# Centring instead of normalising the first four tiles, and moving the queries of chunk 0 to chunk 2, in a linear-attention block with a gated feed-forward network

## The chip, the cores and the metric

The kernel runs on one core of one Trainium2 chip. The metric is the device time of one execution in microseconds (us), and the median over several executions is quoted. The core has these engines: TensorE (PE in the profile, with its weight loads listed apart as PEld), VectorE (DVE), ScalarE (ACT), GpSimd (POOL) and SyncE (SP), whose queue starts almost all the DMA transfers here. The time before the change was 224.95 us (median of 3 runs, 224.90 to 224.96).

## The reference

```python
def reference(A_x, A_wqkv, A_wo, B_x, B_w1, B_w2):     # B_x is not used
    x = A_x                                   # (1, 2048, 640), bf16
    xn = _layernorm(x)                        # (x - mean) / sqrt(var + 1e-5)
    # A: linear attention, 32 heads of 20
    q, k, v = split(xn @ wqkv)                # wqkv (640, 1920)
    phi = lambda t: where(t > 0, t + 1, exp(t)) + 1e-6
    pq, pk = phi(q), phi(k)
    kv  = einsum("bhsd,bhse->bhde", pk, v)
    z   = sum over s of pk
    num = einsum("bhqd,bhde->bhqe", pq, kv)
    den = einsum("bhqd,bhd->bhq", pq, z) + 1e-6
    s   = (num / den) @ wo
    # B: feed-forward network (FFN), 1728 hidden features
    g   = silu(relu(xn @ w1) @ w2)            # w1 (640, 1728), w2 (1728, 640)
    return x + s * g
```

## The kernel before

The 2048 rows of x are 16 tiles of 128 rows, and four tiles make a chunk of 512 rows, so there are four chunks, 0 to 3. TensorE needs the normalised rows with features on the partitions, so each tile is transposed. Tiles 0 to 3 are transposed by TensorE itself in the start, because that is quicker than a DMA. The other tiles are transposed by a DMA. TensorE does three kinds of work on a chunk:

- A query block is five matmuls of 512 columns, and there are five such blocks (640 features). The map phi is applied while the result leaves PSUM: an exponential on ScalarE, then work on VectorE.
- An FFN block is also five matmuls of 512 columns. There are 13 of them, and a last half block of 64 features that two chunks share. Its ReLU is a single ScalarE pass.
- A key block is ten matmuls of 320 columns for one tile of the next chunk. Its evacuation is two ScalarE passes and two VectorE operations; then GpSimd adds the keys to a running sum (`zacc`).

The start normalises tile 0 by way of ScalarE's square root, and tiles 1 to 3 by way of a power on GpSimd:

```python
    def LN_norm(t, then=None):
        last_norm[0] = sc.op("DVE", lambda eng: eng.tensor_scalar(
            out=xn[:, t, :], in0=xin[:, t % XR, :], scalar1=mv[:, t, 0:1], scalar2=rsy[:, t:t + 1],
            op0=ALU.subtract, op1=ALU.mult), R=[("xin", t % XR), ("mv", t), ("rsy", t)], W=[("xn", t)])
        # ... cut: a hook, and the load of tile t + 8

    LN_stat(0, 0); LN_stat(0, 1); LN_aggr(0)
    LN_root_act(0)                       # sqrt on ScalarE
    # ... cut: a dummy Exp on ScalarE, so that its table is loaded early
    LN_stat(1, 0)
    LN_recip(0)
    LN_norm(0, late_loads)
    transposes(0, 4)                     # five transposes by TensorE into PSUM bank 4
    warm(11)                             # dummy matmuls that keep TensorE busy
    xnT_copy(0, 4)                       # ScalarE evacuates them
    LN_stat(1, 1); LN_aggr(1)
    LN_root_pool(1)                      # add and pow on GpSimd
    LN_norm(1)
    LN_stat(2, 0)
    K_mm(0, 0, range(0, KS))             # first part of the key block of tile 0
    transposes(1, 5)
    # ... cut: the same for tiles 2 and 3
```

A query block has two forms of evacuation. In chunk 0 (`j == 0`) ScalarE makes two passes; in the others VectorE reads PSUM itself:

```python
    def Q_block(j, f):
        b = nextb()                      # one of six PSUM banks, in turn
        # ... cut: five matmuls into ps[b]
        sc.op("ACT", ... exp: e_ <- ps[b])
        if j == 0:
            sc.op("ACT", ... relu: r_ <- ps[b])
            sc.op("DVE", ... e_ <- min(e_, 1) + 1e-6)
            sc.op("DVE", ... pqT <- e_ + r_)
            return
        sc.op("DVE", ... r_ <- max(ps[b], 0) + 1e-6)
        sc.op("DVE", ... pqT <- min(e_, 1) + r_)          # scalar_tensor_tensor
```

The chunks run their blocks in one fixed order:

```python
    for j in range(J):
        blocks = [("q", f) for f in range(C)] + [("h", f) for f in range(NF)]
        for n, (kind, f) in enumerate(blocks):
            # ... cut: Q_block or H_block; statistics and norms of the next chunk
            if j + 1 < J:
                if n in (8, 11, 14, 17):
                    t = t0 + (n - 8) // 3
                    K_mm(t, 0)           # key blocks always use PSUM banks 0 and 1
                    K_ev(t, 0)
            else:                        # chunk 3: the sum of the keys and the denominators
                if n == 2: z_split()     # GpSimd
                if n == 7: z_col()       # ten tiny matmuls, then VectorE
                if n == 9:
                    den(); H_half(0); H_half(1)
```

After chunk 3 come 160 matmuls that multiply the normalised rows with the keys (called the product G below), then the second FFN layer and the output. The change hardly touches that part.

## Time and profile before

The profile that came with the kernel was taken in a slow execution. The next fence shows its page: the span, and the shares of the chain of waits that ended last.

```profile
span 464.2 us, 3501 instructions
...
PE 98%; issue 1%; DVE 0%
```

Its chain of waits in order of time shows the pace of TensorE (start, duration, what, count).

```profile
42.47 2.94 PE psT L442 x10
...
45.58 6.83 PE psT L520 x14
```

The execution took 465.64 us against 224.95 us timed. Ten key matmuls (L442) took 2.94 us. In a second profile of the same kernel, which was taken later in the study, they took 1.36 us. The clock column of the slow profile nonetheless read 1.00. Everything that a fast TensorE has to wait for is hidden there. The readings below therefore come from the second profile, which the prediction did not have. That execution took 224.89 us.

| reading (second profile of before) | value |
|---|---|
| span | 223.4 us |
| chunk 0 blocks begin / chunk 1 begins / product G begins | 14.04 / 38.90 / 111.87 us |
| a matmul of 320 / 512 columns, back to back | 0.1358 / 0.2155 us |
| from the product G to the end of the span | 111.55 us |

### The profile page before, as it was taken

The page shows a single profiled execution, that of the slowest core. Times are in us where ns is not written, and L with a number is a line of the kernel's source. Part 1 is how long each engine was busy: PE and PEld are TensorE (multiplying, and loading weights), DVE is VectorE, ACT ScalarE, POOL GpSimd, SP SyncE. Part 2 cuts the span into 40 slices and gives each one's busy share as a digit, 9 for nine tenths or more (in the row PEclk, how much of TensorE's full clock was granted, in tenths as well). Part 3 has the DMA queues.
Part 4 walks back from the last instruction along what each step waited for, and adds up shares of the span by engine and source line. Part 5 has one row for each costly group of instructions (what it writes and reads, how often), then busy time and mean ns, then how long its engine had stood idle before and what let it go on. Part 6 is the DMA issues. An engine that isn't in the chain of part 4 may idle for free.

```text
span 464.2 us, 3501 instructions
## 1 busy us (share of the span) xinstructions
PE 457.0 (98%) x1452; PEld 204.5 (44%) x1462; DVE 99.4 (21%) x192; ACT 91.0 (20%) x146; POOL 44.6 (10%) x63
## 2 busy tenths in 40 slices
PE   9999999999999999999999999999999999999997
PEld 7533333333333333333355556455545554554553
DVE  5580103710064001603000001420202020211141
ACT  4542323232332233222200000220010001001000
POOL 3260111111121112200000002000000000000000
DMA  7850000110002000005496006000000000000020
GB/s 242 287 133 25 1 0 0 34 23 1 1 14 42 0 1 0 0 1 120 105 316 189 0 0 227 0 0 1 29 0 30 0 28 1 28 0 30 0 71 14
DMA packets 24333, 23.18 MB, mean 50 GB/s; under 512 B 9006, under 2 KB 23678, under 8 KB 24318
## 3 DMA queue, kind: packets, MB, share of 16 engines
q1 hardware_dynamic: 24174, 22.88, 16.8%
q8 instruction: 11, 0.18, 0.2%
q10 hardware_dynamic: 144, 0.08, 0.1%
q14 instruction: 4, 0.03, 0.0%
HBM read 15.75 MB, written 5.24 MB: 45 GB/s over the span
## 4 chain that ended last, share of the span: by engine, by line
PE 98%; issue 1%; DVE 0%
PE psT L781 26%; PE psT L520 26%; PE psT L714 10%; PE psT L442 10%; PE psT L497 10%; PE psT L820 9%; PE psT L370 1%; PE psT L742 1%; PE psT L805 1%; PE psT L759 1%; PE psT L533 1%; PE psT L727 1%; PE psT L425 1%; PE psT L619 1%; DVE reg L808 0%
## 5 line engine op out<-in xcount | busy, mean ns | idle before, releaser
L781 PE MATMUL psT<-reg,hT 128*128 128x320 bf16 x416 | 123.3, 502 | 0.3
L520 PE MATMUL psT<-reg 128*128 128x512 bf16 x252 | 120.5, 677 | 2.1 <-issue 2.1
L781 PEld LDWEIGHTS psT<-reg,hT 128*128 128x128 bf16 x416 | 61.2, 148 | 60.4 <-issue 17.8
L520 PEld LDWEIGHTS psT<-reg 128*128 128x128 bf16 x260 | 38.5, 149 | 78.8 <-issue 75.6
L442 PE MATMUL psT<-reg 128*128 128x320 bf16 x160 | 50.2, 504 | 0.0
L524 ACT ACTIVATE hT<-psT 128x512 bf16<-128x512 f32 x52 | 31.0, 597 | 83.8 <-PE psT L520 83.8
L497 PE MATMUL psT<-reg 128*128 128x512 bf16 x98 | 46.6, 679 | 0.6 <-issue 0.6
L714 PE MATMUL psT<-reg 128*128 128x320 bf16 x160 | 46.9, 503 | 0.0
L820 PE MATMUL psT<-reg,pqT 128*128 128x320 bf16 x140 | 42.2, 503 | 0.0
L777 ACT ACTIVATE reg<-psT 128x640 bf16<-128x640 f32 x16 | 10.8, 702 | 149.1 <-PE psT L781 82.2
L834 DVE TENSOR_TENSOR reg<-psT,reg 128x640 bf16<-128x640 f32 x14 | 11.5, 824 | 118.0 <-PE psT L820 118.0
L442 PEld LDWEIGHTS psT<-reg 128*128 128x128 bf16 x160 | 23.1, 146 | 26.2 <-issue 13.7
L714 PEld LDWEIGHTS psT<-reg 128*128 128x128 bf16 x160 | 23.9, 150 | 23.1 <-issue 7.5
L454 POOL TENSOR_TENSOR zacc<-zacc,reg 128x640 f32<-128x640 f32 x16 | 22.5, 1406 | 104.9 <-DVE reg L473 104.6
L820 PEld LDWEIGHTS psT<-reg,pqT 128*128 128x128 bf16 x140 | 20.6, 147 | 20.3 <-issue 6.2
L497 PEld LDWEIGHTS psT<-reg 128*128 128x128 bf16 x100 | 15.2, 152 | 30.1 <-issue 29.4
L471 DVE TENSOR_SCALAR ek<-ek 128x640 bf16<-128x640 bf16 x16 | 5.2, 323 | 102.9 <-ACT ek L459 102.9
L810 POOL TENSOR_TENSOR reg<-reg 128x320 bf16<-128x320 bf16 x1 | 0.8, 788 | 178.3 <-DVE reg L808 178.3
L504 ACT ACTIVATE er<-psT 128x512 bf16<-128x512 f32 x20 | 11.9, 597 | 30.1 <-PE psT L497 30.1
L730 DVE TENSOR_TENSOR reg<-psT,mh 120x120 bf16<-120x120 f32 (+1 forms) x6 | 1.6, 269 | 75.4 <-PE psT L727 75.4
L459 ACT ACTIVATE ek<-psT 128x640 bf16<-128x640 f32 x16 | 11.3, 704 | 30.5 <-PE psT L442 30.5
L386 DVE BATCH_NORM_STATS2 stats<-reg 128x6 f32<-128x320 bf16 x32 | 14.1, 479 | 2.0 <-DMA reg<-in_A_x_dram 2.0
(64 smaller groups left out, 180.8 us busy)
## 6 DMA issues: line engine op xcount, KB each, us to landing
reg<-in_A_x_dram SPq DMA_DIRECT2D x16, 160.0 KB, 5.4
rden_by_feature<-rden SPq DMA_DIRECT2D x4, 640.0 KB, 8.7
reg<-rden_by_feature SPq DMA_DIRECT2D x5, 512.0 KB, 10.1
reg<-in_A_x_dram SPq DMA_DIRECT2D x4, 640.0 KB, 6.2
reg<-in_B_w_dram SPq DMA_DIRECT2D x2, 1120.0 KB, 7.1
out_dram<-reg SPq DMA_DIRECT2D x14, 160.0 KB, 1.8
reg<-in_B_w_dram SPq DMA_DIRECT2D x1, 1040.0 KB, 10.5
reg<-in_B_w_dram SPq DMA_DIRECT2D x1, 960.0 KB, 8.7
```

The costliest lines, as they stand in the source:

```text
L386: sc.op("DVE", lambda eng: eng.bn_stats(stats[:, t, a, :], xin[:, t % XR, HN * a:HN * (a + 1)]), R=[("xin", t % XR)], W=[("stats", t, a)])
L442: fns.append(lambda eng, a=a, k=k: eng.matmul(ps[b + a][:, 0:HN], lhsT=xnT[:, k, tok(t)], rhs=wqk[:, k, D + HN * a:D + HN * (a + 1)], star ...
L454: sc.op("POOL", lambda eng: eng.tensor_tensor(out=zacc[:, :], in0=zacc[:, :], in1=pk[:, t, :], op=ALU.add), R=[("zacc",), ("pk", t)], W=[( ...
L459: sc.op("ACT", lambda eng: eng.activation(out=e_.rearrange("p (a n) -> p a n", a=2), in_=ps2(b, HN), func=ACTF.Exp), R=[("ps", b), ("ps", ...
L497: sc.group("PE", [(lambda eng, k=k: eng.matmul(ps[b], lhsT=wqk[:, k, P * f:P * (f + 1)], rhs=xnT[:, k, schunk(j)], start=(k == 0), stop=(k ...
L504: sc.op("ACT", lambda eng: eng.activation(out=e_, in_=ps[b], func=ACTF.Exp), R=[("ps", b)], W=[("er_e", es)])
L520: a = sc.group("PE", [(lambda eng, k=k: eng.matmul(ps[b], lhsT=w1_sb[:, k, P * f:P * (f + 1)], rhs=xnT[:, k, schunk(j)], start=(k == 0), s ...
L524: sc.op("ACT", lambda eng: eng.activation(out=hT[:, f, schunk(j)], in_=ps[b], func=ACTF.Relu), R=[("ps", b)], W=[("hT", j, f)])
L714: fns.append(lambda eng, t=t, a=a: eng.matmul(ps[b + a][:, 0:HN], lhsT=xn[:, t, P * k:P * (k + 1)], rhs=pk[:, t, HN * a:HN * (a + 1)], sta ...
L781: fns = [(lambda eng, u=u, t=t, f=f, n=n: eng.matmul(ps[bs[n] + u][:, 0:HN], lhsT=hT[:, f, tok(t)], rhs=w2_sb[:, f, HN * n:HN * (n + 1)], ...
L820: sc.group("PE", [(lambda eng, c=c, a=a: eng.matmul(ps[b + a][:, 0:HN], lhsT=pqT[:, c, tok(t)], rhs=wf[:, c, HN * a:HN * (a + 1)], start=( ...
L834: sc.op("DVE", lambda eng: eng.tensor_tensor(out=tmpo[:, os_, lo:hi].rearrange(shp, a=na), in0=src, in1=g_sb[:, t, lo:hi].rearrange(shp, a ...
```

## The change

There are two ideas. First, LayerNorm's division by the standard deviation scales each row by one positive number, so it can be applied after a matmul. Tiles 0 to 3 are only centred before they are transposed, which needs the mean alone. The scale goes into the evacuation of their keys (a scale operand of ScalarE's activation) and, since ReLU keeps positive factors, into the silu of the gate. Second, the queries of chunk 0 need the exponential of fully normalised values and are shared by a whole chunk, so they cannot be scaled that way. They are moved to the end of chunk 2, after tiles 0 to 3 have been normalised and transposed a second time by DMA. Chunk 0 begins with FFN blocks instead. TensorE's matmuls stay the same, apart from six fewer dummies.

```diff
     def late_loads(gate):
-        w_load(wqk[:, :, 0:D], A_wqkv[:, 0:D], ("wq",), extra=[gate])
-        # x tiles 4 to 7, then w1 in two parts
+        for i, (f0, f1) in enumerate(FCUT):                    # w1 in three parts, the first at once
+            w_load(w1_sb[:, :, f0:f1], B_w1[:, f0:f1], ("w1", i), extra=[gate])
+            if i == 0: ...                                     # then x tiles 4 to 7
+        w_load(wqk[:, :, 0:D], A_wqkv[:, 0:D], ("wq",))         # query weights last
+    def LN_center(t):
+        return sc.op("DVE", lambda eng: eng.tensor_scalar(
+            out=xn[:, t, :], in0=xin[:, t % XR, :], scalar1=mv[:, t, 0:1], scalar2=None, op0=ALU.subtract), ...)
+    def K_act(t, b, u, func, key):                             # keys: exp and relu
+        sca, Rs = (rsy[:, t:t + 1], [("rsy", t)]) if t < 4 else (1.0, [])
+        sc.op("ACT", ... activation(..., func=func, scale=sca))
@@ Q_block
-        if j == 0:                                             # the form with two ScalarE passes
-            ...
-            return
@@ the start
-    LN_root_act(0); (dummy Exp); LN_stat(1, 0); LN_recip(0); LN_norm(0, late_loads)
-    transposes(0, 4); warm(11); xnT_copy(0, 4)
-    LN_stat(1, 1); LN_aggr(1); LN_root_pool(1); LN_norm(1); LN_stat(2, 0)
-    K_mm(0, 0, range(0, KS)); transposes(1, 5); xnT_copy(1, 5)
-    ...
+    LN_root(0); late_loads(LN_center(0))                       # the root is off the path now
+    transposes(0, 4); warm(8); xnT_copy(0, 4)
+    LN_stats(1); LN_center(1)
+    transposes(1, 5); xnT_copy(1, 5); K_mm(0, 0, range(0, KS))
+    LN_stats(2); LN_center(2); warm(2)
+    K_mm(1, 2, range(0, KS)); transposes(2, 4); xnT_copy(2, 4)
+    K_mm(0, 0, range(KS, C)); K_exp(0, 0)
+    ...
@@ the chunks
-        blocks = [("q", f) for f in range(C)] + [("h", f) for f in range(NF)]
+    qb = [[], [1], [2, 0], [3]]
+        blocks = [("q", qb[j][0], f) for f in range(C) if j > 0] + [("h", j, f) for f in range(NF)]
+        blocks += [("q", qj, f) for qj in qb[j][1:] for f in range(C)]
+        kat = (6, 8, 10, 12) if j == 0 else (8, 11, 14, 17)    # places of the key blocks
+                    if 8 <= n < 12: LN_norm(n - 8)              # chunk 0: tiles 0 to 3 normalised now
                 if n == 9:
                     den()
-                    H_half(0)
                     H_half(1)
+        if j == 1:
+            H_half(0)
+            for t in range(4): xnT_dma(t)                       # and transposed again
-            if j == 0 and n == 12: ...                             # the load of wv
+            if j == 1 and n == 12: ...                             # one chunk later
@@ silu: with a per-row scale, one tile at a time, for pairs with a tile of 0 to 3
```

More of the change, by code (lines that the diff above doesn't have):

```diff
@@ L339, in bass_recurrent_scan__linear_attn_block__dense_activation_relu__prompt_kernel @@
     KS = 3
+    FCUT = [(0, 4 * P), (4 * P, 9 * P), (9 * P, FF)]
     x_load(0)
@@ L347, in late_loads @@
     def late_loads(gate):
-        w_load(wqk[:, :, 0:D], A_wqkv[:, 0:D], ("wq",), extra=[gate])
-        for t in range(4, XR):
-            x_load(t)
-        F1 = 7 * P
-        w_load(w1_sb[:, :, 0:F1], B_w1[:, 0:F1], ("w1", 0))
-        w_load(w1_sb[:, :, F1:FF], B_w1[:, F1:FF], ("w1", 1))
+        for i, (f0, f1) in enumerate(FCUT):
+            w_load(w1_sb[:, :, f0:f1], B_w1[:, f0:f1], ("w1", i), extra=[gate])
+            if i == 0:
+                for t in range(4, XR):
+                    x_load(t)
+        w_load(wqk[:, :, 0:D], A_wqkv[:, 0:D], ("wq",))
     sc.op("POOL", lambda eng: eng.memset(ident[:], 0.0), W=[("ident",)])
@@ L391, in LN_aggr, with LN_root @@
               R=[("stats", t, 0), ("stats", t, 1)], W=[("mv", t)])
-    def LN_root_pool(t):
+    def LN_root(t):
         sc.op("POOL", lambda eng: eng.tensor_scalar(out=rsv[:, t:t + 1], in0=mv[:, t, 1:2], scalar1=EPS_LN,
@@ L397, in LN_root_pool @@
                                                     op=ALU.pow), R=[("rsv", t), ("mhalf",)], W=[("rsy", t)])
-    def LN_root_act(t):
-        sc.op("ACT", lambda eng: eng.activation(out=rsv[:, t:t + 1], in_=mv[:, t, 1:2], func=ACTF.Sqrt,
-                                                bias=epsv[:, :]), R=[("mv", t), ("epsv",)], W=[("rsv", t)])
-    def LN_recip(t):
-        sc.op("DVE", lambda eng: eng.reciprocal(rsy[:, t:t + 1], rsv[:, t:t + 1]), R=[("rsv", t)], W=[("rsy", t)])
+    def LN_center(t):
+        return sc.op("DVE", lambda eng: eng.tensor_scalar(
+            out=xn[:, t, :], in0=xin[:, t % XR, :], scalar1=mv[:, t, 0:1], scalar2=None, op0=ALU.subtract),
+            R=[("xin", t % XR), ("mv", t)], W=[("xn", t)])
     def LN_stats(t):
@@ L409, in LN_stats @@
         LN_aggr(t)
-        LN_root_pool(t)
+        LN_root(t)
     last_norm = [None]
@@ L455, in z_add @@
               R=[("zacc",), ("pk", t)], W=[("zacc",)])
+    def K_act(t, b, u, func, key):
+        o_ = ek[:, t % NEK, u, :]
+        sca, Rs = (rsy[:, t:t + 1], [("rsy", t)]) if t < 4 else (1.0, [])
+        sc.op("ACT", lambda eng: eng.activation(out=o_.rearrange("p (a n) -> p a n", a=2), in_=ps2(b, HN), func=func,
+                                                scale=sca),
+              R=[("ps", b), ("ps", b + 1)] + Rs, W=[(key, t % NEK)])
     def K_exp(t, b):
-        e_ = ek[:, t % NEK, 0, :]
-        sc.op("ACT", lambda eng: eng.activation(out=e_.rearrange("p (a n) -> p a n", a=2), in_=ps2(b, HN), func=ACTF.Exp),
-              R=[("ps", b), ("ps", b + 1)], W=[("ek_e", t % NEK)])
+        K_act(t, b, 0, ACTF.Exp, "ek_e")
     def K_relu(t, b):
-        r_ = ek[:, t % NEK, 1, :]
-        sc.op("ACT", lambda eng: eng.activation(out=r_.rearrange("p (a n) -> p a n", a=2), in_=ps2(b, HN), func=ACTF.Relu),
-              R=[("ps", b), ("ps", b + 1)], W=[("ek_r", t % NEK)])
+        K_act(t, b, 1, ACTF.Relu, "ek_r")
     def K_fin(t):
@@ L504, in Q_block @@
         sc.op("ACT", lambda eng: eng.activation(out=e_, in_=ps[b], func=ACTF.Exp), R=[("ps", b)], W=[("er_e", es)])
-        if j == 0:
-            sc.op("ACT", lambda eng: eng.activation(out=r_, in_=ps[b], func=ACTF.Relu), R=[("ps", b)], W=[("er_r", es)])
-            sc.op("DVE", lambda eng: eng.tensor_scalar(out=e_, in0=e_, scalar1=1.0, scalar2=1e-6, op0=ALU.min, op1=ALU.add),
-                  R=[("er_e", es)], W=[("er_e", es)])
-            sc.op("DVE", lambda eng: eng.tensor_tensor(out=pqT[:, f, schunk(j)], in0=e_, in1=r_, op=ALU.add),
-                  R=[("er_e", es), ("er_r", es)], W=[("pqT", j, f)])
-            return
         sc.op("DVE", lambda eng: eng.tensor_scalar(out=r_, in0=ps[b], scalar1=0.0, scalar2=1e-6, op0=ALU.max, op1=ALU.add),
@@ L522, in H_block @@
                                                          start=(k == 0), stop=(k == C - 1))) for k in range(C)],
-                     R=[("w1", 0 if f < 7 else 1)] + [("xnT", 4 * j + q) for q in range(4)], W=[("ps", b)])
+                     R=[("w1", 0 if f < 4 else 1 if f < 9 else 2)] + [("xnT", 4 * j + q) for q in range(4)], W=[("ps", b)])
         sc.op("ACT", lambda eng: eng.activation(out=hT[:, f, schunk(j)], in_=ps[b], func=ACTF.Relu),
@@ L535, in H_half @@
                     start=(k == 0), stop=(k == C - 1)))
-        a = sc.group("PE", fns, R=[("w1", 1)] + [("xnT", 8 * jp + q) for q in range(8)], W=[("ps", b)])
+        a = sc.group("PE", fns, R=[("w1", 2)] + [("xnT", 8 * jp + q) for q in range(8)], W=[("ps", b)])
         sc.op("ACT", lambda eng: eng.activation(out=hTl[:, jp, :], in_=ps[b], func=ACTF.Relu),
@@ L544, in bass_recurrent_scan__linear_attn_block__dense_activation_relu__prompt_kernel @@
     LN_aggr(0)
-    LN_root_act(0)
-    sc.op("ACT", lambda eng: eng.activation(out=junk[:, :], in_=epsv[:, :], func=ACTF.Exp), R=[("epsv",)], W=[("junk",)])
-    sc.allow_unread.add(("junk",))
-    LN_stat(1, 0)
-    LN_recip(0)
-    LN_norm(0, late_loads)
+    LN_root(0)
+    late_loads(LN_center(0))
     transposes(0, 4)
-    warm(11)
+    warm(8)
     xnT_copy(0, 4)
-    LN_stat(1, 1)
-    LN_aggr(1)
-    LN_root_pool(1)
-    LN_norm(1)
-    LN_stat(2, 0)
-    K_mm(0, 0, range(0, KS))
+    LN_stats(1)
+    LN_center(1)
     transposes(1, 5)
     xnT_copy(1, 5)
-    LN_stat(2, 1)
-    LN_aggr(2)
-    LN_root_pool(2)
+    K_mm(0, 0, range(0, KS))
+    LN_stats(2)
+    LN_center(2)
     warm(2)
+    K_mm(1, 2, range(0, KS))
+    transposes(2, 4)
+    xnT_copy(2, 4)
     K_mm(0, 0, range(KS, C))
@@ L568, in bass_recurrent_scan__linear_attn_block__dense_activation_relu__prompt_kernel @@
     LN_stats(3)
-    LN_norm(2)
-    warm(3)
-    K_mm(1, 2, range(0, 2))
-    transposes(2, 4)
-    xnT_copy(2, 4)
-    LN_norm(3)
-    K_mm(1, 2, range(2, C))
+    LN_center(3)
+    K_mm(1, 2, range(KS, C))
+    K_mm(2, 6, range(0, 2))
     transposes(3, 5)
@@ L578, in bass_recurrent_scan__linear_attn_block__dense_activation_relu__prompt_kernel @@
     K_relu(0, 0)
-    K_mm(2, 6)
+    K_mm(2, 6, range(2, C))
     K_exp(1, 2)
@@ L635, in bass_recurrent_scan__linear_attn_block__dense_activation_relu__prompt_kernel @@
     lastW1 = None
+    qb = [[], [1], [2, 0], [3]]
     for j in range(J):
-        blocks = [("q", f) for f in range(C)] + [("h", f) for f in range(NF)]
-        for n, (kind, f) in enumerate(blocks):
+        blocks = [("q", qb[j][0], f) for f in range(C) if j > 0] + [("h", j, f) for f in range(NF)]
+        blocks += [("q", qj, f) for qj in qb[j][1:] for f in range(C)]
+        kat = (6, 8, 10, 12) if j == 0 else (8, 11, 14, 17)
+        for n, (kind, bj, f) in enumerate(blocks):
             if kind == "q":
-                Q_block(j, f)
+                Q_block(bj, f)
             else:
-                lastW1 = H_block(j, f)
+                lastW1 = H_block(bj, f)
             if j + 1 < J:
@@ L653, in bass_recurrent_scan__linear_attn_block__dense_activation_relu__prompt_kernel @@
                         xnT_dma(7)
+                    if 8 <= n < 12:
+                        LN_norm(n - 8)
                 else:
@@ L659, in bass_recurrent_scan__linear_attn_block__dense_activation_relu__prompt_kernel @@
                         xnT_dma(t0 + n // 2)
-                if n in (8, 11, 14, 17):
-                    t = t0 + (n - 8) // 3
+                if n in kat:
+                    t = t0 + kat.index(n)
                     K_mm(t, 0)
@@ L676, in bass_recurrent_scan__linear_attn_block__dense_activation_relu__prompt_kernel @@
                     den()
-                    H_half(0)
                     H_half(1)
-            if j == 0 and n == 12:
+            if j == 1 and n == 12:
                 w_load(wv_sb[:, :, :], A_wqkv[:, 2 * D:3 * D], ("wv",))
+        if j == 1:
+            H_half(0)
+            for t in range(4):
+                xnT_dma(t)
     for a in range(2):
@@ L775, in silu @@
         def silu(n):
+            dv = [divs[c] for c in sorted({v // S for t in (t0, t1) for v in (D * t, D * t + D - 1)})]
+            if t0 < 4:
+                for u, t in enumerate((t0, t1)):
+                    sca, Rs = (rsy[:, t:t + 1], [("rsy", t)]) if t < 4 else (1.0, [])
+                    sc.op("ACT", lambda eng, u=u, t=t, sca=sca: eng.activation(
+                        out=g_sb[:, t, HN * n:HN * (n + 1)], in_=ps[bs[n] + u][:, 0:HN], func=ACTF.Silu, scale=sca),
+                        R=[("ps", bs[n] + u)] + Rs, W=[("g", t, n)], extra=dv)
+                return
             go = g_sb[:, t0:t0 + 5:4, HN * n:HN * (n + 1)]
             sc.op("ACT", lambda eng: eng.activation(out=go, in_=ps2(bs[n], HN), func=ACTF.Silu),
-                  R=bk(n), W=[("g", t0, n), ("g", t1, n)], extra=[divs[c] for c in sorted({v // S for t in (t0, t1) for v in (D * t, D * t + D - 1)})])
+                  R=bk(n), W=[("g", t0, n), ("g", t1, n)], extra=dv)
         for n in range(2):
```

## The prediction

> **What bounds the kernel now.** The page's chain of waits is TensorE for 98% of the 464.2 us profiled span. But the profiled execution took 465.64 us against 224.95 us timed. In its timeline ten 320-column matmuls take 2.94 us and fourteen 512-column ones 6.71 us, near 1.2 GHz pace, clock column 1.00. So the profile hides waits that only a fast TensorE meets; I halve TensorE and keep other engines, DMA landings and waits.
>
> Summing columns over the groups (no dummy matmuls or transposes) gives about 493,000. The Trainium skill, "TensorE: Matmul & The Clock Gate", section "Back-to-back issue gap", gives N/2.4 + 2.5 ns; some 1,300 matmuls make an estimated 209 us. The profile is slower, so no trace here confirms this. Of 225 us only about 16 are left: the start, a 3.2 us tail (last matmul to end), few stalls. TensorE's real work stays, so only the start can be won.
>
> **Start, before (timeline).** Tile 0's mean is there at 4.10, then root (0.29) and reciprocal (0.16), normalised at 5.11, transposed at 5.33, evacuated 6.14-6.84. Tile 1 waits 1.00 us of VectorE idle for the GpSimd root (rsv 0.23, pow 0.57), tile 3 waits 0.72; tiles 1 to 3 are normalised at 7.20, 9.69 and 10.86. Halving TensorE in this order by hand, first key matmuls at 7.0, key stage done near 14.2. Loads land in time: key weights 7.7, query 11.9, FFN 16.6 and 19.6.
>
> **After.** Centring needs the mean alone: tiles 0 to 3 near 4.55, 6.1, 7.95, 9.5. Tile 0 gains little, because the 38 dummy matmuls run to 5.3-5.5. The sqrt table load leaves (1.28 us twice becomes once; the skill, "ScalarE: Activation LUTs", "What ACT_TABLE_LOAD costs", says 1283 ns, and the trace agrees); it should run before any data, since the old one did not wait for its input. Tiles 1 to 3 no longer wait for GpSimd, and six dummy matmuls go. By hand the key stage ends near 13.1: minus 1.1 us, all critical.
>
> FFN blocks first in chunk 0: one 0.60 us ScalarE pass per 1.09 us block, instead of 1.19 us ScalarE plus VectorE work that stretched to 1.5 us an operation beside GpSimd's zacc adds (28-34 us). Eight banks mostly hid this; I give 0.4 us. First FFN weights should land by 11.
>
> Costs: ten query blocks in a row from chunk 2 into 3, VectorE 1.38 us each against 1.09: a lag of 3-5 us, held by six banks, 0-0.5 us exposed. Eight two-tile gates become sixteen half ones (0.70 becomes two of 0.44 plus); ScalarE idles there. Four 0.45 us normalisations and four transposing DMAs (2.6 us) fall in slack. Total costs 0.2.
>
> **Predicted: 223.7 us, range 222.4 to 225.0.** Faster by over 2%: 0.05; within 2%: 0.93; slower: 0.02.
>
> **What would show it.** Centring within 0.1 us after each mean, no VectorE wait on the GpSimd root in tiles 0-3; one table load before the first evacuation; last key matmuls of tile 3 earlier; TensorE never waiting at chunk 0's first FFN block or at chunk 3's start. The profile, with slow TensorE, may show less or another gain than the timed runs.
>
> **What would make it wrong.** The table load landing between transposes and first evacuation (+1.3 us); fewer dummy matmuls leaving TensorE at a slow clock longer (+1 us or more); the ten-query run stalling TensorE by several us; or chunk 0's query evictions having stalled the old kernel more than I think, a larger gain (to -3 us).

## More of the kernel before

The section starts are read from the timeline. Where the trace lacks the first record of a row of matmuls (24 of 25 shown, for instance), one back-to-back step was subtracted. The timeline of the start follows (start, duration, engine, line, operation, tensors, count; in brackets the idle time before it and what ended it).

```profile
4.00 0.21 DVE L390 BATCH_NORM_AGGREGATE mv<-stats 128x2 f32<-128x12 f32 x1
...
4.25 0.29 ACT L400 ACTIVATE rsv<-mv,epsv 128x1 f32<-128x1 f32 x1 [1.24 <-DVE mv L390]
4.56 1.28 ACT L546 ACT_TABLE_LOAD   x1
...
4.78 0.45 DVE L415 TENSOR_SCALAR reg<-reg,mv,rsy 128x640 bf16<-128x640 bf16 x1
...
6.71 0.99 PE L442 MATMUL psT<-reg 128*128 128x320 bf16 x6 [0.36 <-ACT reg L430]
6.88 0.45 DVE L415 TENSOR_SCALAR reg<-reg,mv,rsy 128x640 bf16<-128x640 bf16 x1 [1.01 <-POOL rsy L396]
...
9.87 0.45 PE L425 MATMUL psT<-ident,reg 128*128 128x128 bf16 x5 [0.39 <-DVE reg L415]
```

Tile 0's mean is ready at 4.21, but its normalised rows (L415) come at 4.78 to 5.23, after the root and its reciprocal. Tile 1 costs VectorE a wait of 1.01 us for GpSimd's power. TensorE (L442 and L425) then waits for these results.

The chain of waits of the same profile around the last chunk shows no such gaps.

```profile
88.78 5.39 PE psT L497 x25
...
94.23 3.19 PE psT L520 x14
97.42 0.23 PE psT L606 x10
97.65 2.18 PE psT L520 x10
99.83 1.19 PE psT L619 x20
101.02 2.28 PE psT L533 x20
...
103.46 8.58 PE psT L520 x39
112.04 21.73 PE psT L714 x160
```

These are, in turn: five query blocks, three FFN blocks, the sum of the keys (L606), two FFN blocks, the denominators (L619), both half blocks together (L533), eight FFN blocks, and the product G. The busy times in chunk 0 say the same (stretch, length, then busy microseconds and counts of PE, PEld, DVE, ACT, POOL, then the clock, the DMA share and GB/s):

```profile
14.04:38.90 24.86, 24.70 (x129) 12.72 (x130) 17.65 (x37) 18.39 (x33) 14.44 (x15) 1.00 0.61 169
```

PE is busy for 24.70 of 24.86 us. The blocks of the chunk need 90 matmuls of 512 columns and 40 of 320, and 90 × 0.2155 + 40 × 0.1358 = 24.83 us. Chunk 0 of the kernel before was therefore as dense as it can be.

## The result and the profile after

The changed kernel took 224.66 us (median of 6 runs, 224.41 to 225.20) against 224.93 us (6 runs, 224.84 to 224.96). The ratio was 0.9990, with a 95% interval of 0.9977 to 1.0003. A ratio here is the mean time of one kernel's fast runs over that of the other kernel's in the same rounds, so it is not quite the ratio of the two medians. The gain was 0.27 us where 1.25 us had been forecast, and the interval includes no gain at all. The profile after, first its page (span, and shares of the chain):

```profile
span 223.0 us, 3502 instructions
...
PE 91%; DVE 7%; ACT 1%; issue 1%; DVEq 0%
```

VectorE now has 7% of the chain, against 3% in the second (full-pace) profile of the kernel before. The timeline of the start in the kernel after (same columns) shows what the centring did.

```profile
0.80 1.28 ACT L430 ACT_TABLE_LOAD   x1 [0.80 <-PEq L908]
...
4.06 0.21 DVE L391 BATCH_NORM_AGGREGATE mv<-stats 128x2 f32<-128x12 f32 x1
...
4.30 0.39 DVE L402 TENSOR_SCALAR reg<-reg,mv 128x640 bf16<-128x640 bf16 x1
...
6.63 0.97 PE L442 MATMUL psT<-reg 128*128 128x320 bf16 x6
...
6.94 0.89 DVE L387 BATCH_NORM_STATS2 stats<-reg 128x6 f32<-128x320 bf16 x2 [0.79 <-DMA reg<-in_A_x_dram]
...
13.29 1.89 PE L516 MATMUL psT<-reg 128*128 128x512 bf16 x8
```

Centring (L402) follows each mean within 0.1 us, and VectorE waits for no root any more. The one table load of the start ran at 0.80, before any data. The next limit is the load of x: the statistics of tile 2 (L387) waited 0.79 us for its DMA. The first FFN matmul (L516; this view was cut at 15 us) stands at 13.29. The chain of waits counts 34 of 35 matmuls in that row, so one record is missing at its head, and the row began one step earlier, at 13.07, against 14.04 before.

The busy times in chunk 0 of the kernel after (columns as before):

```profile
13.07:32.53 19.46, 19.36 (x105) 10.27 (x105) 17.15 (x32) 14.28 (x24) 14.07 (x15) 1.00 0.68 178
```

Its blocks need 65 × 0.2155 + 40 × 0.1358 = 19.44 us, so this chunk, too, is as dense as it can be. It could not be denser than it had been, and five query blocks have only moved.

In chunk 3 the picture changed. This is the timeline of the kernel after around the ten query blocks in a row.

```profile
85.73 1.40 POOL L454 TENSOR_TENSOR zacc<-zacc,reg 128x640 f32<-128x640 f32 x1 [3.20 <-DVE reg L476]
...
86.31 1.38 DVE L510 SCALAR_TENSOR_TENSOR pqT<-er 128x512 bf16<-128x512 bf16 x1
...
90.91 0.60 ACT L507 ACTIVATE er<-psT 128x512 bf16<-128x512 f32 x1 [1.15 <-DVE pqT L510]
...
92.06 0.68 DVE L508 TENSOR_SCALAR er<-psT 128x512 bf16<-128x512 f32 x1
...
92.77 0.69 DVE L510 SCALAR_TENSOR_TENSOR pqT<-er 128x512 bf16<-128x512 bf16 x1
...
98.10 0.76 PEld L516 LDWEIGHTS psT<-reg 128*128 128x128 bf16 x5 [0.21 <-DVE er L508]
...
99.43 0.76 PEld L516 LDWEIGHTS psT<-reg 128*128 128x128 bf16 x5 [0.57 <-DVE er L508]
```

VectorE needs 0.68 + 0.69 us for a query block, and TensorE makes one every 5 × 0.2155 = 1.08 us. Five in a row, as before, are absorbed by the PSUM banks; ten are not. The first L510 even took 1.38 us. The Trainium skill, "SBUF — State Buffer", section "SBUF: two separate sides", says that VectorE and GpSimd share a pair of ports as an exclusive lock and that the loser blocks. The trace agrees here: the operation began at 86.31 while GpSimd added keys until 87.13, and it ended 0.56 us after that, somewhat under its usual 0.69 us. ScalarE (L507) must then wait for VectorE to free one of three buffers, and the weight loads of two FFN blocks wait for banks (0.21 and 0.57 us). In the matmuls themselves each of these two waits shows as a gap of 0.26 us, 0.52 us in all.

The chain of waits of the kernel after, from there on, runs through VectorE:

```profile
98.78 0.61 DVE er L508
...
99.43 1.25 PE psT L516 x5
100.68 1.19 PE psT L606 x20
101.88 1.20 PE psT L529 x10
...
103.24 8.58 PE psT L516 x39
111.82 21.73 PE psT L709 x160
```

By the timelines the product G began at 111.65, against 111.87. From there to the end of the span it is 111.33 us against 111.55. So 0.97 us were won in the start, and all but 0.22 us of them were lost between chunk 1 and the product G. (Section lengths are good to about 0.01 us.)

| section of TensorE, us | before | after | difference |
|---|---|---|---|
| start, to the first block of chunk 0 | 14.04 | 13.07 | −0.97 |
| chunk 0 | 24.86 | 19.46 | −5.40, of which five query blocks are 5.39 |
| chunk 1 to the product G | 72.97 | 79.12 | +6.15, of which five query blocks are 5.39 |
| product G to the end of the span | 111.55 | 111.33 | −0.22 |
| time outside the profiled span, mean of all runs | 1.45 | 1.73 | +0.28 |

The last row is the device time minus the span. It was 1.40 to 1.53 us in 38 fast runs of the kernel before and of the half-block experiment below, and 1.68 to 1.80 us in 62 runs of kernels that contain the change. So 0.28 us of the span's gain does not reach the timed gain, and no run isolates which part of the change costs it. Nor were the −0.22 us of the row above it won by TensorE: its last row of matmuls begins 106.57 us after the product G, against 106.54 before. They lie behind the last matmuls, and their cause was not looked for.

The open question for the experiments was what the 6.15 − 5.39 = 0.76 us are, and which part of the change earned the 0.97 us.

### The profile page after: what moved, and what is told of

It reads as the page before. It is cut to its first block, busy times and chain, and to the rows that moved or that the text cites. A ratio compares the mean times of both kernels' runs of the same rounds, so it can differ in the third digit from the quotient of the medians.

```text
span 223.0 us, 3502 instructions
## 1 busy us (share of the span) xinstructions
PE 217.6 (98%) x1446; PEld 134.6 (60%) x1456; DVE 107.9 (48%) x195; ACT 86.2 (39%) x146; POOL 46.8 (21%) x65
## 4 chain that ended last, share of the span: by engine, by line
PE 91%; DVE 7%; ACT 1%; issue 1%; DVEq 0%
PE psT L784 26%; PE psT L516 23%; PE psT L442 10%; PE psT L709 10%; PE psT L823 9%; PE psT L500 5%; DVE pqT L510 3%; DVE er L508 3%; PE psT L371 2%; PE psT L737 1%; PE psT L808 1%; PE psT L754 1%; PE psT L529 1%; PE psT L425 1%; PE psT L722 1%; ACT ek L460 1%
## 5 line engine op out<-in xcount | busy, mean ns | idle before, releaser
L784 PE MATMUL psT<-reg,hT 128*128 128x320 bf16 x416 | 58.7, 299 | 0.3
L516 PE MATMUL psT<-reg 128*128 128x512 bf16 x253 | 57.7, 379 | 0.7 <-issue 0.2
L784 PEld LDWEIGHTS psT<-reg,hT 128*128 128x128 bf16 x416 | 40.3, 98 | 17.0 <-PE psT L754 1.6
L516 PEld LDWEIGHTS psT<-reg 128*128 128x128 bf16 x260 | 25.2, 98 | 29.5 <-DVE er L508 0.8
L442 PE MATMUL psT<-reg 128*128 128x320 bf16 x160 | 24.4, 299 | 0.0
L500 PE MATMUL psT<-reg 128*128 128x512 bf16 x97 | 21.8, 379 | 0.2
L709 PE MATMUL psT<-reg 128*128 128x320 bf16 x160 | 21.9, 299 | 0.0
L780 ACT ACTIVATE reg<-psT 128x640 bf16<-128x640 f32 x8 | 5.4, 702 | 39.4 <-PE psT L784 20.6
L442 PEld LDWEIGHTS psT<-reg 128*128 128x128 bf16 x160 | 15.4, 98 | 8.0 <-ACT reg L430 0.3
L823 PE MATMUL psT<-reg,pqT 128*128 128x320 bf16 x140 | 20.0, 299 | 0.0
L709 PEld LDWEIGHTS psT<-reg 128*128 128x128 bf16 x160 | 15.7, 98 | 6.2
L460 ACT ACTIVATE ek<-psT 128x640 bf16<-128x640 f32 x24 | 15.6, 701 | 9.1 <-PE psT L442 9.1
L823 PEld LDWEIGHTS psT<-reg,pqT 128*128 128x128 bf16 x140 | 13.7, 98 | 5.3
L500 PEld LDWEIGHTS psT<-reg 128*128 128x128 bf16 x100 | 9.7, 98 | 11.6 <-issue 0.4
L507 ACT ACTIVATE er<-psT 128x512 bf16<-128x512 f32 x20 | 12.0, 598 | 10.6 <-DVE pqT L510 5.5
L387 DVE BATCH_NORM_STATS2 stats<-reg 128x6 f32<-128x320 bf16 x32 | 14.1, 481 | 2.9 <-DMA reg<-in_A_x_dram 2.9
L510 DVE SCALAR_TENSOR_TENSOR pqT<-er 128x512 bf16<-128x512 bf16 x20 | 15.0, 750 | 0.7
```

The lines of the kernel that those rows point to most:

```text
L387: sc.op("DVE", lambda eng: eng.bn_stats(stats[:, t, a, :], xin[:, t % XR, HN * a:HN * (a + 1)]), R=[("xin", t % XR)], W=[("stats", t, a)])
L442: fns.append(lambda eng, a=a, k=k: eng.matmul(ps[b + a][:, 0:HN], lhsT=xnT[:, k, tok(t)], rhs=wqk[:, k, D + HN * a:D + HN * (a + 1)], star ...
L460: sc.op("ACT", lambda eng: eng.activation(out=o_.rearrange("p (a n) -> p a n", a=2), in_=ps2(b, HN), func=func, scale=sca), R=[("ps", b), ...
L500: sc.group("PE", [(lambda eng, k=k: eng.matmul(ps[b], lhsT=wqk[:, k, P * f:P * (f + 1)], rhs=xnT[:, k, schunk(j)], start=(k == 0), stop=(k ...
L507: sc.op("ACT", lambda eng: eng.activation(out=e_, in_=ps[b], func=ACTF.Exp), R=[("ps", b)], W=[("er_e", es)])
L510: sc.op("DVE", lambda eng: eng.scalar_tensor_tensor(out=pqT[:, f, schunk(j)], in0=e_, scalar=1.0, in1=r_, op0=ALU.min, op1=ALU.add), R=[(" ...
```

## The experiments

All outputs are right. Differences of a few tenths of a microsecond are small beside the spread between runs, so the section lengths in the traces carry the argument, and the times only check it. Two theories stood against each other for the lost gain. Theory A: the long row of query blocks backs up behind VectorE, and TensorE loses time in chunk 3. Theory B: the loss lies in chunk 0, where key blocks wait for transposing DMAs that now run behind other loads. Later a third came: the half block of the FFN, split off, costs time by itself. The expectations use other letters: their theory S is the start's gain together with theory A, and R, T and U are rivals to it.

The expected times were mostly missed, and nearly always by being too low. The spread queries (223.9 expected, 224.55 measured) landed in the range given to the rival; ScalarE's evacuation (224.37) fell between the two ranges; the later sum of the keys came at 224.44 instead of 224.1, undone centring at 228.40 instead of 225.3 to 225.8, and both edits together at 224.61 instead of 223.9. The later key blocks and the earlier tile 2, which might have gained 0.1 to 1 us, gained nothing. The load of the query weights made no difference, as its rival had it. What came as expected were the section lengths in chunk 3, the difference of about 0.5 us between the last two kernels with and without spreading, and the cost of the split half block. None of the expectations allowed for the 0.28 us outside the span.

### The kernel before at full pace

There was no edit.

> The kernel before, unedited, for a profile at full TensorE speed (the first one was taken at half speed). Theory S (start won, given back later): the first FFN or query matmul of chunk 0 starts near 14.2 us here, against 13.1 us in the changed kernel, and TensorE runs from chunk 2 into chunk 3 without the 0.8 us or so of gaps that the changed kernel shows around 98 to 103 us. Theory R (rival, nothing to win): the old key stage ends within 0.4 us of the new one (13.3 to 13.6 us) although its normalised tiles come later, and the gaps around chunk 3 are the same in both.

It took 224.89 us, with a clock of 1.00 and a span of 223.4 us. This is the profile shown above as the second one. A matmul of 320 columns steps by 0.1358 us and one of 512 by 0.2155 us. The Trainium skill, "TensorE: Matmul & The Clock Gate", section "Back-to-back issue gap", gives N / 2.4 + 2.5 ns, which is 135.8 and 215.8 ns. The trace agrees.

### The late queries spread out among FFN blocks

```diff
         blocks += [("q", qj, f) for qj in qb[j][1:] for f in range(C)]
+        if j == 2:
+            late = blocks[-C:]
+            blocks = blocks[:-C]
+            for at, late_q in zip((9, 12, 15, 18, 20), late):
+                blocks.insert(at, late_q)
```

> The changed kernel with chunk 0's five query blocks put between chunk 2's FFN blocks (as blocks 9, 12, 15, 18 and 20 of its 23) instead of all after them, just ahead of chunk 3's five. Theory S (the start won 1.0 us, a run of ten query blocks at VectorE's pace gave back about 0.75): the gaps in TensorE's matmuls at 97.8 and 99.0 us and the waits at the denominator vanish, 223.9 us (223.7 to 224.1), and runs differ less than 0.2 us. Rival T (the small gaps there are not what costs; the loss lies in late loads or the split gates of the last stage): stays within 0.2 us of the changed kernel, 224.5 to 224.8.

It took 224.55 us (5 runs, 223.99 to 224.71) against 224.94, ratio 0.9977 (0.9964 to 0.9990). Chunk 1 to the product G took 78.60 us instead of 79.12. The chain of this kernel around chunk 3 runs through TensorE alone again:

```profile
91.68 3.19 PE psT L500 x14
94.87 3.24 PE psT L516 x15
98.10 0.23 PE psT L593 x10
98.33 2.18 PE psT L516 x10
```

So 0.52 us came back in the trace, as theory A says. The time alone did not show it: 224.55 us is not clearly below the changed kernel's 224.66. They were run at other times. Its own profile also had a wait in chunk 0, before the first key block, from its timeline:

```profile
20.98 1.52 PE L442 MATMUL psT<-reg 128*128 128x320 bf16 x10 [0.36 <-DMA reg<-reg]
```

Chunk 0 took 19.98 us instead of 19.46. Theory B's mechanism is therefore real in some executions, but the profile of the changed kernel shown above did not have it (19.46 us, dense).

### The late queries evacuated by ScalarE, as before

Here the form with two ScalarE passes was put back for the queries of chunk 0, in their new place.

```diff
+        if j == 0:
+            # e_ <- exp, r_ <- relu on ScalarE; then two bf16 operations on VectorE
+            return
```

> The changed kernel with the old evacuation for chunk 0's queries alone: relu by ScalarE, VectorE left with two 16-bit operations of 0.29 and 0.43 us instead of 0.69 and 0.69. The ten blocks stay in a row. Theory S with VectorE's backlog as the cause: VectorE gets 5 x 0.66 = 3.3 us less to do before chunk 3, so its lag at the end of the run is gone and the time falls to 223.9 to 224.2 us. Rival U (the order of blocks itself, or GpSimd's split of z slowing VectorE, costs): at least half of the loss stays, 224.4 or more.

It took 224.37 us (5 runs, 224.04 to 224.51) against 224.94, ratio 0.9972 (0.9961 to 0.9984). Chunk 1 to the product G took 78.60 us again, with ten query blocks still in a row. This is the cleanest test of theory A, as nothing but the evacuation of five blocks has changed. A block costs VectorE 0.28 + 0.42 = 0.70 us this way, instead of 1.37, where GpSimd is not adding; three of the ten operations overlapped GpSimd's and took 0.80 to 1.58 us. In sum the five late blocks held VectorE for 6.1 us instead of 8.0. The waits between 83 and 104 us show it, first those of the changed kernel (engine and line, waited for, total, times, longest):

```profile
ACT er L507 <- DVE pqT L510: 4.1, 5, 1.2
```

and then those of this experiment, where VectorE's line is L512:

```profile
ACT er L507 <- DVE pqT L512: 0.7, 1, 0.7
```

### The sum of the keys and the denominators two blocks later

```diff
-                if n == 7:
+                if n == 9:
                     z_col()
-                if n == 9:
+                if n == 11:
                     den()
```

> The changed kernel with the column of z moved two FFN blocks later in chunk 3 (block 9 instead of 7) and the denominator too (11 instead of 9). If TensorE lost its time only because z and the denominator wait at the end of VectorE's queue, two blocks (2.2 us) more let the queue drain: about 0.4 to 0.6 us less, 224.1 us. If instead the PSUM banks of the late query blocks are what FFN blocks wait for, the gaps stay at the FFN blocks and it gains at most 0.2 us. A risk: the reciprocals reach the divides 2.2 us later, which had next to no slack, so a wait could arise there.

It took 224.44 us (6 runs, 224.29 to 225.39) against 224.94, ratio 0.9988 (0.9973 to 1.0003). Chunk 1 to the product G took 78.60 us here too. Nothing of the VectorE backlog was removed; only its consumers came later, when it had been worked off. In this trace five FFN blocks ran behind the row without a wait. So the backlog costs time through the sum of the keys and the denominators close behind it. Chunk 0 of this profile took 20.13 us: the key block of tile 4 waited for its transposing DMA.

### Centring undone, the new order kept

Tiles 0 to 3 are fully normalised in the new order of the start, and the later scales, norms and second transposes are dropped.

```diff
     def LN_center(t):
-            ..., scalar1=mv[:, t, 0:1], scalar2=None, op0=ALU.subtract)
+            ..., scalar1=mv[:, t, 0:1], scalar2=rsy[:, t:t + 1], op0=ALU.subtract, op1=ALU.mult)
-        ... if t < 4 ...        # scale in the key evacuation
+        ... if t < 0 ...        # never; the same in silu
-                        LN_norm(n - 8)
+                        x_load(n)
-            for t in range(4): xnT_dma(t)
```

> The changed kernel with the centring undone alone: tiles 0 to 3 normalised in full before their transposes, the root by GpSimd for all four, key and gate scales 1, no second normalisation and no later transposing DMAs; block order, loads, key-stage order as in the change. If the start's 1.0 us comes from centring: tile 0 waits for the root (0.42 and 0.57 us), every tile comes about 1 us later, first FFN block at 13.9 to 14.3 us instead of 13.1, and the time is 225.3 to 225.8 us. If the start's gain came from the new order of the key stage and six dummy matmuls fewer: within 0.3 us of the changed kernel.

It took 228.40 us (4 runs, 228.23 to 228.51) against 224.94, ratio 1.0153 (1.0139 to 1.0166). Chunk 0 began at about 16.54 instead of 13.07. Two lines of its timeline show the beginning:

```profile
5.34 0.45 DVE L402 TENSOR_SCALAR reg<-reg,mv,rsy 128x640 bf16<-128x640 bf16 x1 [1.00 <-POOL rsy L397]
...
8.33 0.59 PE L425 MATMUL psT<-ident,reg 128*128 128x128 bf16 x5 [1.59 <-DVE reg L402]
```

VectorE waited 0.99 or 1.00 us for the root of each of the four tiles, and TensorE stood idle for 1.59 us. The busy times of this kernel in three stretches (columns as before; the clock is the third number from the end) show what followed.

```profile
...
8.30:10.00 1.70, 1.67 (x10) 1.15 (x11) 0.97 (x3) 0.70 (x1) 0.52 (x2) 0.56 1.08 385
10.00:11.60 1.60, 1.60 (x9) 0.97 (x8) 1.26 (x4) 0.00 (x0) 0.27 (x1) 0.50 1.06 378
12.30:14.00 1.70, 1.70 (x18) 1.24 (x15) 0.60 (x2) 1.30 (x2) 0.45 (x1) 1.00 1.07 391
```

The granted clock fell to 0.56 and 0.50 after the gap and was back at 1.00 by 12.3; in between a key matmul took 0.267 us a step instead of 0.136. The Trainium skill, "TensorE: Matmul & The Clock Gate", section "Why this matters for your kernels", asks for no idle gaps over about 3 us. Here the clock fell after a gap of 1.59 us with one of 0.59 us ahead of it; whether the longer one alone would have done it is not shown. So the cost of this experiment is larger than the chain of operations alone, and it must not be read as "centring is worth 3.5 us": the old kernel had another order, with more dummies.

### The old order with centring

Here the new centring is kept, and TensorE's order and the dummies of the start are the old ones.

```diff
-    warm(8)
+    warm(11)
     LN_stats(1)
     LN_center(1)
+    K_mm(0, 0, range(0, KS))
     transposes(1, 5)
     xnT_copy(1, 5)
-    K_mm(0, 0, range(0, KS))
     # ... cut: tiles 2 and 3 likewise; warm(3) and K_mm(1, 2, range(0, 2)) back
```

> The changed kernel with centring, but the key stage on TensorE in the old order and with the old 16 filling dummies: key block 0 ahead of tile 1's transposes. If centring alone won the start: chunk 0 starts at 13.0 to 13.2 us as in the change, 224.5 to 224.8 us. If the order is needed too: TensorE waits again about 0.5 us for the first evacuation before key block 0, chunk 0 starts at 13.6 to 13.9 us and the time is 225.0 to 225.4 us, no better than the kernel before.

It took 225.51 us (5 runs, 225.46 to 225.66) against 224.96, ratio 1.0026 (1.0014 to 1.0038), which is slightly slower. Chunk 0 began at 13.96, so centring with the old order gained 0.1 us of the 0.97. The timeline shows why.

```profile
6.98 0.97 PE L442 MATMUL psT<-reg 128*128 128x320 bf16 x6 [0.60 <-DMA reg<-in_A_wqkv_dram]
```

In the old order the first key matmuls stand before the transposes of tile 1, so a late load of the key weights stops TensorE. In the new order the transposes come first. The loads were late in this trace (tile 2 of x at 7.29 us); in the changed kernel such a landing went with a chunk 0 that began near 13.45, so at equal landing the new order is worth an estimated 0.5 us (13.45 is 7.29 plus the 6.16 us given in the account of the prediction below). The two experiments together say that the 0.97 us need both: centring without the new order gained 0.1 us, and the new order without centring lost. The order and the six dummies were changed together here, so they are not told apart.

### The key blocks of chunk 0 one block later

```diff
-        kat = (6, 8, 10, 12) if j == 0 else (8, 11, 14, 17)
+        kat = (7, 9, 11, 12) if j == 0 else (8, 11, 14, 17)
```

> The changed kernel with the key blocks of tiles 4 to 7 one block later in chunk 0 (after blocks 7, 9, 11, 12 instead of 6, 8, 10, 12). In two of four traces of the new order TensorE waited 0.45 to 0.67 us for tile 4's transposing DMA, which stands behind the query weights in the queue. If that wait is a part of the loss: no wait before tile 4's key block, and the median falls from 224.66 by 0.1 to 0.4 us, with the slow runs (225.2) gone. If it is only two unlucky traces: 224.5 to 224.7 as before. The 0.52 us of gaps in chunk 3 must stay.

It took 225.20 us (5 runs, 225.02 to 225.54) against 224.96, ratio 1.0013 (1.0001 to 1.0025). Chunk 1 to the product G was 79.10 us, as in the changed kernel. Chunk 0 took 19.95 us, because the edit made a wait of its own:

```profile
31.78 1.53 PE L442 MATMUL psT<-reg 128*128 128x320 bf16 x10 [0.31 <-ACT ek L460]
```

The last two key blocks share PSUM banks 0 and 1 and had only one FFN block between them, so TensorE waited for ScalarE. This try at theory B was spoilt by its own design.

### Both edits, and the load of tile 2 earlier

One kernel joined the spreading with the later key blocks. Another added to it that tile 2 of x is loaded ahead of the key weights, because tile 2 was the new limit of the start.

```diff
     x_load(1)
-    w_load(wqk[:, 0:KS, D:2 * D], A_wqkv[0:P * KS, D:2 * D], ("wk", 0))
     x_load(2)
+    w_load(wqk[:, 0:KS, D:2 * D], A_wqkv[0:P * KS, D:2 * D], ("wk", 0))
```

> Both cures: chunk 0's query blocks spread over chunk 2, and the key blocks one block later. If the two losses add: 223.9 us (223.6 to 224.2), 0.4 to 0.5% under the kernel before. If TensorE's total is set elsewhere, by the start's own spread from run to run: about 224.4, like spreading alone (224.55).

> Both cures, and tile 2 of x loaded before the first key weights. In the new start VectorE waits 0.54 to 1.16 us for tile 2 (landed 6.67 to 7.25 us, behind 480 KB of weights), where the old start waited for GpSimd's root. If that landing is now what sets the start: tile 2 is centred by 7.2 us instead of 8.1, its transposes no longer wait, and chunk 0 starts near 12.6 us instead of 13.1, 223.5 us. If the weights' landing (6.3 to 6.8 us, now 0.4 us later) is as tight, it only moves the wait to the first key block: no change to within 0.2 us.

The first took 224.61 us (5 runs, 224.51 to 224.88) against 224.96, ratio 0.9988 (0.9976 to 1.0000). Chunk 1 to the product G was 78.59 us and chunk 0 was 19.95. The second took 225.07 us (6 runs, 224.58 to 225.78), ratio 1.0008 (0.9995 to 1.0022), so the earlier load did not help. Its chunk 0 began at 13.00 against 12.85. Tile 2 came earlier, but the first key block then waited for weights that landed at 6.61. The start is bounded by what the queue has brought by about 7 us, and reordering two loads only moves the wait.

### The query weights loaded later

If the transposing DMA of tile 4 is late because the query weights stand ahead of it in the queue, they can go behind it.

```diff
     def late_loads(gate):
-        w_load(wqk[:, :, 0:D], A_wqkv[:, 0:D], ("wq",))
     # ... cut: the key stage, to
     xnT_dma(5)
+    w_load(wqk[:, :, 0:D], A_wqkv[:, 0:D], ("wq",))
```

> The changed kernel with the query weights (wanted only in chunk 1) issued after tile 5's transposing DMA instead of ahead of both. If tile 4's key block waits for its transpose only because 800 KB of weights stand before it in the queue: the transpose lands near 19 us instead of 20.4 to 21.4, the key block at 20.4 us never waits, chunk 0 is dense (19.5 us) in the profile, and the median is 0.1 to 0.4 us under that of the changed kernel beside it, with a spread under 0.4 us. If the wait was rare: no difference beyond 0.1 us.

> The same, and chunk 0's query blocks spread over chunk 2. If the terms add: 0.5 us under the e9_wqlater beside it, 223.8 us (223.5 to 224.2), below both kernels and the best of this study. If spreading gains nothing beyond it: the same as e9_wqlater.

> The changed kernel again, unedited, on the chip of the other three: 224.4 to 225.2 us, median 224.6 to 224.9, spread wider than that of the kernel before, from the start's loads and tile 4's transpose.

The second label is the same edit together with the spreading, and the third is the changed kernel as it is, run beside both on one chip. They took 224.94 (224.79 to 225.03), 224.45 (223.98 to 224.70) and 224.92 us (224.60 to 225.15), 5 runs each, against 224.90 for before. The ratios were 1.0002 (0.9988 to 1.0016), 0.9979 (0.9966 to 0.9991) and 1.0001 (0.9989 to 1.0014). Three things follow.

- Theory B does not explain the lost gain: 224.94 with the load moved against 224.92 without it is no difference in the medians. In the profiles its wait was there in some executions (0.52 and 0.67 us in chunk 0, in two of the seven traces that left this load and the key blocks in place) and not in others. How often it struck in the runs that were not profiled stays open.
- Theory A holds in the times, too: spreading alone separates 224.45 from 224.94, which is 0.49 us, and the traces say 0.52.
- On this chip the changed kernel was no faster than before, 224.92 against 224.90. Its profile nonetheless read 12.86 at the start and 79.11 for chunk 1 to the product G. Two things go into this: the profile is of the fastest of the five runs (224.60), and the median span was 0.3 us shorter than that of the kernel before (223.2 against 223.5), which the longer time outside the span took back.

### The half block split off, in the kernel before

In the kernel before both half blocks run together. The change pulls the first forward to the end of chunk 1. Here only that was done, to the kernel before.

```diff
                 if n == 9:
                     den()
-                    H_half(0)
                     H_half(1)
+            if j == 1 and n == len(blocks) - 1:
+                H_half(0)
```

> The kernel before, with the 64-column block of chunks 0 and 1 moved to the end of chunk 1, away from that of chunks 2 and 3 (as the change has it). If entering and leaving such a block costs TensorE about 0.1 us each time, as the trace of the change shows: 0.2 to 0.3 us slower than the kernel before, 225.15 to 225.2. If not: within 0.05 us.

It took 225.09 us (5 runs, 225.08 to 225.18) against 224.90, ratio 1.0010 (0.9997 to 1.0022). Chunk 1 to the product G took 73.19 us against 72.97, so the split cost 0.22 us, and the times say 0.19. The chain shows both halves and the block after the first.

```profile
64.00 1.20 PE psT L533 x10
65.20 5.50 PE psT L497 x25
...
102.40 1.20 PE psT L533 x10
```

Together the two halves had taken 2.28 us; apart they take 1.20 each, which is 0.12 more. The query blocks after the first took 5.50 us instead of 5.39, which is 0.11 more. The sum, 0.23, is close to the 0.22 of the section. Why a block with 64-column weights costs this at its edges is not shown by any run.

## Why the prediction was wrong

The time fell in the range, and so did "within 2%", but the forecast of −1.25 us was more than four times the measured −0.27. It was a sum of three terms. Two of them failed: the 0.4 us for chunk 0 measured 0.0, and the 0.2 us of costs measured 0.74. A further 0.28 us, outside the profiled span, stood in no term.

| term | predicted, us | measured, us | shown by |
|---|---|---|---|
| start | −1.1 | −0.97 | section starts in both profiles |
| chunk 0 with FFN blocks first | −0.4 | 0.0 | both chunks as long as their matmuls |
| costs | +0.2 | +0.74 | 0.52 (row of ten query blocks) and 0.22 (split half block); the sections left 0.76 |
| product G to the end of the span | none | −0.22 | section lengths; cause open |
| outside the profiled span | none | +0.28 | time minus span, all runs; cause open |
| sum | −1.3 | −0.17 | −0.18 between the two profiled executions, −0.27 in the medians |

- **"By hand the key stage ends near 13.1: minus 1.1 us, all critical."** This was right in size and in mechanism, though it took the loads to land in time, and in the changed kernel the landing of tile 2 of x became the limit. The start of chunk 0 moved from 14.04 (14.12 in the half-block experiment) to 13.08, the mean of nine traces with the new start, which range from 12.82 to 13.43. It was also right that the table load would run before the data and that the dummy matmuls could be fewer. What the prediction did not say is that centring needs the new order of TensorE's work: with the old order it gained 0.1 us.
- **"I give 0.4 us" for FFN blocks first in chunk 0.** This step failed. The chunk before took 24.86 us where its matmuls need 24.83. ScalarE was busy for 18.39 of 24.86 us and VectorE for 17.65, and TensorE hardly waited for either. The prediction saw VectorE operations stretched to 1.5 us in the slow profile and guessed at a loss; but the profile with TensorE at half pace could not show whether a fast one would wait, and a count of the matmuls against the chunk's length was not to be had.
- **"Ten query blocks in a row […] 0-0.5 us exposed", in "Total costs 0.2".** This was the right mechanism, with the size at its upper end: 0.52 us. Three edits removed it (spreading, ScalarE's evacuation, later consumers), and each gave 78.60 instead of 79.12 us. Why it was more than a small part: the prediction took six banks as the buffer, but ScalarE was held by three buffers of its output, GpSimd stretched two of VectorE's operations to 1.38 and 1.17 us, and the sum of the keys and the denominators needed banks and VectorE right behind. Only the last of these three was tested by itself.
- **The split half block was not in the sum.** The diff shows one moved line and no added matmul, and the prediction gave it no cost. It cost 0.22 us.
- **The costs in the gate.** The prediction saw these as slack, and TensorE's last row of matmuls comes only 0.03 us later after the product G. The Trainium skill, "ScalarE: Activation LUTs", section "What ACT_TABLE_LOAD costs", gives about 93 ns for each pointer operand. The trace agrees: a half pass of the gate took 0.53 us with the per-row scale and 0.43 without (medians of eight), and the first key evacuation 0.79 us against 0.70.

The spread of the start (0.6 us from trace to trace) has a source that the traces show. In all nine, chunk 0 begins 6.16 us after tile 2 of x lands, and that landing ranges from 6.67 to 7.28 us; in the kernel before and the half-block experiment it was 6.17 and 6.71, and chunk 0 did not follow it (7.88 and 7.41 us later). The start therefore goes with this one load now; where it was brought forward (tile 2 first), the key weights took its place. What stays open is why its landing varies and whether the change itself makes it later, what the 0.28 us outside the span are, and how often the transposing DMA of tile 4 delayed a key block. The combination of the change with ScalarE's evacuation (224.37 us) or with the spreading and the later load (224.45 us) beats the kernel before in its own call, by 0.57 and 0.45 us. That is 0.3 and 0.2%. The second also beat the changed kernel beside it; the first was not run beside it.

## What to carry to other kernels

Before crediting a new order with a denser stage, multiply the stage's matmuls by their measured step and compare the sum with the stage's length: where the two agree, reordering can win nothing there, and it can only move work next to something that cannot absorb it. When work is moved, look at the per-block time of every engine that serves it over the whole new row, at each buffer in its path, and at what stands directly behind the row. Compare time minus span as well as spans: a gain inside the profile can be lost outside it. A profile in which the busiest engine ran at half pace says what the work is, but not where that engine waits at full pace, so take one at full pace before you cost small waits.

## What the Trainium skill lacked or had wrong

- "TensorE: Matmul & The Clock Gate", section "Back-to-back issue gap", gives about 131 ns per matmul of 512 columns as the sustained pace of a stream of weight loads and matmuls, and says that N / 2.4 + 2.5 ns counts too much there. In these runs each matmul had its own weight load, and the step was 215.5 ns, which is the formula's value.
- The same page, section "Why this matters for your kernels", warns of idle gaps over about 3 us. Early in a kernel, an idle gap of 1.59 us (after one of 0.59 us) was followed by a granted clock of 0.50 to 0.56 for about 3 us, and the kernel took 3.5 us longer than before the change, its waits included.
- No page that I found gives a whole execution with TensorE at about half pace while the granted clock in the profile reads 1.00: 465.64 us against 224.95 us for the same kernel. The skill's warning that clock records can be unreliable comes near it. The column read 1.00 in the first 5 us of the full-pace profiles too, where the dummy matmuls of 128 columns stepped by 0.107 us, against 0.056 us from about 5.5 us on; the drop to half in the run without centring it did show. The step of the matmuls is the surer sign.
- No page that I found gives the cost in time of entering and leaving a block of matmuls whose weights have 64 columns (the page on array packing speaks of a drain at a change of tiling mode, without a figure). Splitting one such pair in two cost 0.22 us (73.19 against 72.97 us).
